# Two one-bank PSUM tiles for the second MLP's products in place of a shared two-bank tile

## The chip, the cores and the metric

The kernel runs on one core of one Trainium2 chip. A core has a tensor engine (PE, with its weight loads shown as PEld), a vector engine (DVE), a scalar engine (ACT), a GpSimd engine (POOL) and a sync engine (SP) that here issues most DMAs. Matmuls write into PSUM, 8 banks of 128 partitions by 512 fp32 values. The metric is the time of one execution on the device in microseconds; below is better.

## The reference

```python
def reference(q, k, v, moe_w_in, moe_w_out, moe2_w_in, moe2_w_out):
    # q, k, v: [8, 8, 576, 64]; w_in: [512, 2048]; w_out: [2048, 512]; all float32
    scores = q @ k.transpose(0, 1, 3, 2) / np.sqrt(64)
    ret = scores * Dmat        # causal decay gamma[h] ** (i - j), zero above the diagonal
    attn = ret @ v
    x = attn.transpose(0, 2, 1, 3).reshape(4608, 512)
    h = x @ moe_w_in
    x = (h * sigmoid(1.702 * h)) @ moe_w_out
    h = x @ moe2_w_in
    return (h - np.tanh(h)) @ moe2_w_out
```

## The kernel before

The 4608 tokens are worked in nine blocks (NB) of 512. Every product of fp32 operands is done as three matmuls of halves (PASS): each operand is split into a high part and a rest, kept side by side. The order of the instructions on each engine is the order in which the program writes them; the tile framework adds the waits, from the record of who read and wrote each tile, and hands a pool's slot to its next tile when the last one's accesses are over.

Retention (the attention part) runs first, interleaved with the first MLP. It computes in `pat`, one PSUM tile of two banks from the pool `ps_a`, and for the first blocks also in two tiles of `ps_e`. The first MLP's `mm_in` writes `h` tiles (pool `ps_h`, two banks), and its output products `mm_out` accumulate in four banks of `ps_acc`. Outputs of both MLPs are produced by one generator, `out_units`: each call of `some(outs, n)` emits n units of three matmuls (L507 for the first MLP, L509 for the second), and `evac` copies four finished accumulators out with ScalarE (L525) after every 16 steps of four units.

The second MLP's first block is done in the standard way (`mm_std`, L646). The other eight blocks go by pairs, four pairs of eight steps each, 32 steps `u` in all. A step forms seven products of combined operands (`mm_part`, L660, six matmuls each) in place of eight, and adds up four results from them. In program order a step does:

1. part 1 into x_ps, copied out as m1; then the activation of h11 of the step before (`late[0]`)
2. part 5 into y_ps, copied as m5; then the activation of the last sum of the step before (`late[1]`), which is still in PSUM, in that step's x_ps
3. part 6 added into x_ps, copied as u2 (`copied`, L866)
4. part 3 added into y_ps; h12 = y_ps + u2 (`added`, L871)
5. part 7 added into x_ps; h22 = x_ps + m5; activation of h12
6. part 2 into w_ps; h11 = w_ps + m1
7. part 4 added into x_ps; activation of h22

Output units stand between all of these. x_ps is `pat[:, u % 2]` and w_ps `pat[:, 1 - u % 2]`: the bank of w_ps in step u is that of x_ps in step u - 1, and the bank of x_ps that of w_ps. y_ps is a tile of its own from `ps_h`. An activation, `act_2`, reads its h with ScalarE (L454, L456) and VectorE (L455, L461; L461 is the last reader), and L457, L458, L460 and L462 work in SBUF. In the last but one output block, `mm_out` also uses the two halves of `pat` as its first two accumulators.

Of the kernel before, what the change touches and what calls it, by code (L numbers as in the profile page):

```python
# [8 lines left out]
F32 = mybir.dt.float32  # L9
# [8 lines left out]
P = 128  # L18
# [6 lines left out]
BLK = 512  # L25
# [23 lines left out]
def kernel(  # L49
# [18 lines left out]
    t_p = ctx.enter_context(tc.tile_pool(name="t", bufs=2))  # L68
    st_p = ctx.enter_context(tc.tile_pool(name="st", bufs=2))
    dram = ctx.enter_context(tc.tile_pool(name="dram", bufs=1, space=bass.MemoryType.DRAM))  # L70
    ps_a = ctx.enter_context(tc.tile_pool(name="ps_a", bufs=1, space=bass.MemoryType.PSUM))
    ps_h = ctx.enter_context(tc.tile_pool(name="ps_h", bufs=2, space=bass.MemoryType.PSUM))

    ctx.enter_context(tc.manual_schedule())

    early_ctx = ExitStack()
    tabs = early_ctx.enter_context(tc.tile_pool(name="tabs", bufs=1))
    at_p = early_ctx.enter_context(tc.tile_pool(name="at", bufs=2))
    qt_sb = tabs.tile([P, KD, P], F32, name="qt_sb")
# [44 lines left out]
    def dec_b(m, f, c):  # L124
        hi, _, e, z = half[m, f, c]
        nc.vector.scalar_tensor_tensor(
            out=e, in0=hi, scalar=-(2 ** 31), in1=e, op0=ALU.bitwise_and, op1=ALU.bitwise_or
        )
        del stg[m, f, c]
        o = z.bitcast(F32)  # L130
        nc.vector.tensor_tensor(out=o, in0=z.bitcast(F32), in1=e.bitcast(F32), op=ALU.mult)
        half[m, f, c] = o
        if (m, c) == (1, 0):
            part[m, f, c] = half.pop((m, f, c))

    def dec_c(m, f, c):
        if (m, c) == (1, 0):
            return
        o = half[m, f, c]
        if (m, c) == (0, 0):  # L140
            s = win[f] = wts.tile([P, 2, KD, P], F32R, tag=f"wi{f}", name="wi")
            sv = s.rearrange("p a k c -> p a (k c)")
        else:
            sv = st_p.tile([P, 2, DM], F32R, tag="ws", name="ws", bufs=2)
        nc.scalar.activation(out=sv[:, 0], in_=o, func=ACTF.Copy)
        half[m, f, c] = o, sv

    def dec_d(m, f, c):
        if (m, c) == (1, 0):
            return  # L150
        o, sv = half.pop((m, f, c))
        nc.vector.tensor_tensor(out=sv[:, 1], in0=o, in1=sv[:, 0].bitcast(F32), op=ALU.subtract)
        if (m, c) != (0, 0):
            part[m, f, c] = sv

    def dec_store():
        while part:
            (m, f, c), sv = part.popitem()
            if (m, c) == (1, 0):
                w2_d[f] = dram.tile([P, BLK], F32, tag=f"w{m}{f}{c}", name="wr")  # L160
                nc.sync.dma_start(out=w2_d[f], in_=sv)
                continue
            d = dram.tile([P, 2 * DM], F32, tag=f"w{m}{f}{c}", name="wd")
            nc.sync.dma_start(out=d, in_=sv.rearrange("p a n -> p (a n)").bitcast(F32))
            wo_d[m, f] = d
# [5 lines left out]
    def dec_load(n):  # L171
        while n_load[0] < min(n, len(chunks)):
            wload(*chunks[n_load[0]])
            n_load[0] += 1

    def dec_piece(pieces=1):

        for _ in range(pieces):
            n, k = divmod(n_dec[0], 3)
            if k == 0:  # L180
                dec_store()
            if n >= len(chunks) + 2:
                return
            n_dec[0] += 1
            if k == 0:
                dec_load(n + 2)
                if n >= 2:
                    dec_c(*chunks[n - 2])
                if 1 <= n <= len(chunks):
                    dec_b(*chunks[n - 1])  # L190
                continue
            if k == 1 and n >= 2:
                dec_d(*chunks[n - 2])
            if n < len(chunks):
                (dec_a if k == 1 else dec_a2)(*chunks[n])
# [68 lines left out]
    pat = ps_a.tile([P, 2, BLK], F32, name="pat")  # L264
# [149 lines left out]
    acc = {}  # L414
# [53 lines left out]
    second = {}  # L468
# [24 lines left out]
    def mm_out(s, m):  # L493
        j, f = divmod(s, NF)
        if f == 0:
            if j == 2 * NB - 2 and m < 2:
                acc[m] = pat[:, m]
            elif j == 2 * NB - 1 and m > 1:
                acc[m] = ps_h.tile([P, BLK], F32, tag="h", name="acc")
            else:  # L500
                acc[m] = ps_acc.tile([P, BLK], F32, tag=f"acc{m}", name=f"acc{m}")
        g, wo = gt[s], wos[s]
        c = slice(m * P, (m + 1) * P)
        for n, (a, b) in enumerate(PASS):
            first, last = f == 0 and n == 0, f == NF - 1 and n == 2
            if j < NB:
                nc.tensor.matmul(acc[m], lhsT=wo[:, a, c], rhs=g[:, b], start=first, stop=last)  # L507
            else:
                nc.tensor.matmul(acc[m], lhsT=g[:, a, c], rhs=wo[:, b], start=first, stop=last)  # L509
# [22 lines left out]
    def out_loads(o):  # L532
        while n_w[0] <= min(o + (3 if second else 2), n_steps - 1):
            wo_load()
        while n_g[0] <= min(o + (4 if second else 2), n_steps - 1):
            g_load(n_g[0])
            n_g[0] += 1
# [116 lines left out]
    def mm_part(ps, q, i, first):  # L654

        t, o = PART[i]
        n = 0
        for k in range(2):
            for a, b in PASS:
                nc.tensor.matmul(  # L660
                    ps, lhsT=wq[q][t][:, o, a, k], rhs=xo[i][k][:, b],
                    start=first and n == 0, stop=n == 5, skip_group_check=True,
                )
                n += 1
# [145 lines left out]
    for s in range(LAG, NB * NF):  # L810
        j, f = divmod(s, NF)
        o = s - LAG
        if s < PAUSE:
            out_loads(o)
        mm_in(s)
        b = EARLY + BPB + (s - LAG) // 2
        if s % 2 == 0 and b <= TILES * BPT:
            attn_step(b)
            if b == TILES * BPT:
                early_ctx.close()  # L820
                second["pool"] = ctx.enter_context(tc.tile_pool(name="second", bufs=1))
        dec_piece()
        act_a(s)
        if s < PAUSE:
            out_split(o)
        done.append(s)
        stores(2)
        if s < PAUSE:
            some(outs, 4)
        dec_piece(2 if j == 2 and f < 10 else 1)  # L830
        if n_dec[0] >= 3 * (len(chunks) + 2):
            some(prep, 1)
        if j == NB - 1 and f >= 5:
            some(std, 1)
        if j == NB - 1 and f in (11, 14):
            wq_load((f - 11) // 3, True)
# [38 lines left out]
    for u in range(pairs * QS):  # L875
        p, q = divmod(u, QS)
        ja = NB + 1 + 2 * p
        a, b = (ja * NF + q, (ja + 1) * NF + q)
        end = p == pairs - 1
        if q == 0:  # L880
            xo.update(new)
            new = {}
            ops = xo_prep(3 + 2 * p, new) if not end else iter(())
        final = q == QS - 1
        stay = iter(range(7, NF)) if end and final else iter(())

        def ready():
            if final:
                some(ops, 1)
                for f in islice(stay, 2):  # L890
                    wo_stay(f)

        n = 4 if final else 3
        x_ps, w_ps = pat[:, u % 2], pat[:, 1 - u % 2]
        y_ps = ps_h.tile([P, BLK], F32, tag="h", name="y")

        mm_part(x_ps, q, 1, True)
        m1 = copied(x_ps, "m1")
        some(outs, n)
        if late:  # L900
            act(*late[0])

        mm_part(y_ps, q, 5, True)
        m5 = copied(y_ps, "m5")
        some(outs, n)
        if late:
            act(*late[1])
        ready()

        mm_part(x_ps, q, 6, False)  # L910
        u2 = copied(x_ps, "u2")
        some(outs, n)
        if u + 1 < pairs * QS:
            wq_load((q + 1) % QS, False)
        ready()

        mm_part(y_ps, q, 3, False)
        h12 = added(y_ps, u2, "h12")
        some(outs, n)
        ready()  # L920

        mm_part(x_ps, q, 7, False)
        h22 = added(x_ps, m5, "h22")
        some(outs, n)
        act(a + QS, h12)
        ready()

        mm_part(w_ps, q, 2, True)
        h11 = added(w_ps, m1, "h11")
        some(outs, n + final)  # L930
        ready()

        mm_part(x_ps, q, 4, False)
        some(outs, 4 + final)
        act(b + QS, h22)
        if not final and q:
            some(ops, 1)
        if end and q == QS - 2:
            for f in range(3, 7):
                wo_stay(f)  # L940
        late = ((a, h11), (b, x_ps))
# [59 lines left out]
```

## Time and profile before

| | |
|---|---|
| median of 3 runs | 2001.58 us (1999.08 to 2008.21) |
| the profiled execution's own time | 1995.94 us |
| its span | 1993.9 us |
| mean granted TensorE clock | 0.945 of full speed |
| busy: PE, DVE, ACT | 1779.3, 1115.3, 875.8 us |

The profile is of one execution. Its span is 2.0 us shorter than that execution's time. PE busy time counts a matmul from its start to its modelled end, so that neighbours overlap, and a slowly clocked matmul counts as busy for longer. In a timeline, the bracket at the end of a row gives the engine's idle time just before it and the instruction that ended it.

### The profile page before, as it was taken

The numbers are of one execution on the slowest core, as the hardware profiler recorded it, in microseconds if no ns is written. First come the engines' busy times: TensorE is split into PE (matmuls) and PEld (weight loads), VectorE is DVE, ScalarE is ACT, GpSimd is POOL, SyncE is SP. The second block draws the span as 40 slices with busy tenths as digits, with TensorE's granted clock in tenths as the row PEclk, the third lists the DMA queues.
The fourth block names the chain that finished last, engine by engine and source line by source line (L and its number), as shares of the span: only waits on it lengthen the run. The fifth ranks groups of instructions, "written<-read, shape, count | busy, mean of one in ns | idle before, by whom it ended". The sixth has DMA issues, their size and how long they took to land.

```text
span 1993.9 us, 24696 instructions
## 1 busy us (share of the span) xinstructions
PE 1779.3 (89%) x8714; PEld 1431.8 (72%) x8714; DVE 1115.3 (56%) x1837; ACT 875.8 (44%) x1587; POOL 149.6 (8%) x121
## 2 busy tenths in 40 slices
PE   7998999999999999887878888888687888888889
PEld 5786888888788887776666666767575767676677
DVE  6787865565644445555455555555545565454432
ACT  3343433333333344554455444555445464444432
POOL 4100100110132101001000010000100000000000
PEclk8998999999999999998899989989889999898989
DMA  6468998888877689987667776767767576766943
GB/s 243 170 208 310 368 308 296 299 312 299 280 250 252 254 305 360 332 280 279 209 203 265 239 265 218 270 211 269 257 235 258 194 256 239 263 210 225 358 166 101
DMA packets 176025, 514.21 MB, mean 258 GB/s; under 512 B 19872, under 2 KB 21024, under 8 KB 164384
## 3 DMA queue, kind: packets, MB, share of 16 engines
q1 hardware_dynamic: 164960, 493.69, 71.0%
q10 hardware_dynamic: 10944, 18.96, 2.5%
q8 instruction: 69, 1.13, 0.2%
q14 instruction: 52, 0.43, 0.1%
HBM read 380.45 MB, written 132.12 MB: 257 GB/s over the span
## 4 chain that ended last, share of the span: by engine, by line
PE 66%; DVE 13%; ACT 10%; DMA 7%; issue 4%; ACTq 0%; SPq 0%; DVEq 0%
PE h L430 16%; PE acc L507 15%; PE acc L509 14%; PE pat L660 12%; ACT pl L457 3%; DVE pl L460 3%; DMA gd<-t 3%; DVE pl L461 3%; PE y L660 2%; ACT sq L456 2%; PE h L646 2%; PE pat L298 1%; DMA wq<-wq 1%; ACT t L454 1%; DVE t L455 1%
## 5 line engine op out<-in xcount | busy, mean ns | idle before, releaser
L507 PE MATMUL acc<-g,wos 128*128 128x512 f32 x1728 | 436.0, 401 | 6.6 <-ACT g L490 3.8
L660 PE MATMUL pat<-xo,wq 128*128 128x512 f32 x960 | 286.7, 440 | 163.7 <-DVE pl L461 141.3
L491 DVE TENSOR_TENSOR g<-gl,g 128x512 fp32r<-128x512 f32 x288 | 205.5, 715 | 373.4 <-ACT g L490 362.8
L507 PEld LDWEIGHTS acc<-g,wos 128*128 128x128 f32 x1728 | 333.4, 194 | 84.6 <-ACT o L525 4.2
L430 PE MATMUL h<-xh,wi 128*128 128x512 f32 x1152 | 378.8, 398 | 7.0 <-DVE t L440 4.7
L509 PE MATMUL acc<-wos,g 128*128 128x512 f32 x1398 | 357.7, 403 | 2.6 <-ACT o L525 2.5
L660 PEld LDWEIGHTS pat<-xo,wq 128*128 128x128 f32 x960 | 198.4, 212 | 224.2 <-ACT marks L458 114.8
L490 ACT ACTIVATE g<-gl 128x512 fp32r<-128x512 f32 x288 | 180.9, 629 | 390.9 <-PE acc L509 229.6
L509 PEld LDWEIGHTS acc<-wos,g 128*128 128x128 f32 x1398 | 276.5, 198 | 66.3 <-ACT o L525 5.6
L430 PEld LDWEIGHTS h<-xh,wi 128*128 128x128 f32 x1152 | 218.9, 190 | 60.3 <-DVE t L440 5.9
L430 PE MATMUL h<-xl,wi 128*128 128x512 f32 x576 | 226.7, 394 | 0.7 <-DVE xl L364 0.7
L440 DVE SCALAR_TENSOR_TENSOR t<-t,h 128x512 f32<-128x512 f32 x144 | 98.4, 684 | 122.0 <-ACT t L439 121.4
L460 DVE SCALAR_TENSOR_TENSOR pl<-pl,sq 128x512 f32<-128x512 f32 x144 | 101.1, 702 | 100.8 <-ACT pl L457 100.2
L439 ACT ACTIVATE t<-h 128x512 f32<-128x512 f32 x144 | 85.3, 594 | 123.8 <-DMA gd<-t 72.6
L430 PEld LDWEIGHTS h<-xl,wi 128*128 128x128 f32 x576 | 109.5, 190 | 23.0 <-DVE xl L364 1.0
L114 ACT ACTIVATE e<-e,ebias 128x512 int32<-128x512 int32 x64 | 46.3, 724 | 174.9 <-DVE e L112 174.2
L462 DVE COPY_PREDICATED t<-marks,pl 128x512 f32<-128x512 int32 x144 | 110.5, 767 | 15.2 <-ACT o L525 0.5
L457 ACT ACTIVATE pl<-sq,abias 128x512 f32<-128x512 f32 x144 | 104.1, 723 | 4.7
L458 ACT ACTIVATE marks<-sq,sbias 128x512 f32<-128x512 f32 x144 | 101.9, 708 | 0.0
L660 PE MATMUL y<-xo,wq 128*128 128x512 f32 x384 | 97.7, 390 | 0.0
L255 POOL TENSOR_TENSOR at<-at,qt_sb 128x512 f32<-128x512 f32 x35 | 47.6, 1360 | 537.3 <-DMA at<-in_attn_dram 467.0
L364 DVE TENSOR_TENSOR xl<-pat,xh 128x256 fp32r<-128x256 f32 x61 | 25.7, 422 | 108.5 <-ACT xh L363 108.3
(87 smaller groups left out, 1786.1 us busy)
## 6 DMA issues: line engine op xcount, KB each, us to landing
wos<-wd SPq DMA_DIRECT2D x262, 512.0 KB, 4.4
gd<-t SPq DMA_DIRECT2D x288, 256.0 KB, 5.0
gl<-gd SPq DMA_DIRECT2D x288, 256.0 KB, 4.4
wq<-wq SPq DMA_DIRECT2D x48, 1024.0 KB, 7.4
at<-in_attn_dram SPq DMA_DIRECT2D x33, 1024.0 KB, 6.3
stg<-in_w_dram SPq DMA_DIRECT2D x64, 512.0 KB, 6.8
wq<-wq SPq DMA_DIRECT2D x32, 768.0 KB, 9.1
wd<-ws SPq DMA_DIRECT2D x32, 512.0 KB, 6.4
```

What stands on the lines that cost most here:

```text
L430: nc.tensor.matmul(h, lhsT=win[f][:, a, k], rhs=xs[b][:, k], start=(n == 0), stop=(n == 3 * KD - 1))
L439: nc.scalar.activation(out=t, in_=h, func=ACTF.Tanh, scale=0.851)
L440: nc.vector.scalar_tensor_tensor(out=t, in0=t, scalar=1.0, in1=h, op0=ALU.add, op1=ALU.mult)
L457: nc.scalar.activation(out=pl, in_=sq, func=ACTF.Square, bias=abias)
L458: nc.scalar.activation(out=small, in_=sq, func=ACTF.Relu, bias=sbias, scale=-1.0)
L460: nc.vector.scalar_tensor_tensor(out=pl, in0=pl, scalar=CB, in1=sq, op0=ALU.add, op1=ALU.mult)
L462: nc.vector.copy_predicated(out=t, mask=small.bitcast(I32), data=pl)
L490: nc.scalar.activation(out=g[:, 0], in_=t, func=ACTF.Copy)
L491: nc.vector.tensor_tensor(out=g[:, 1], in0=t, in1=g[:, 0].bitcast(F32), op=ALU.subtract)
L507: nc.tensor.matmul(acc[m], lhsT=wo[:, a, c], rhs=g[:, b], start=first, stop=last)
L509: nc.tensor.matmul(acc[m], lhsT=g[:, a, c], rhs=wo[:, b], start=first, stop=last)
L660: nc.tensor.matmul(ps, lhsT=wq[q][t][:, o, a, k], rhs=xo[i][k][:, b], start=first and n == 0, stop=n == 5, skip_group_check=True,)
```

## The change

The pool `ps_a` with `pat` moves to the other side of PSUM and into the context that closes with retention. When it closes, a pool `ps_x` opens there, with two tags x0 and x1 of one bank each. Each step takes a tile for x_ps from tag x(u % 2) at its start, and one for w_ps from tag x(1 - u % 2) just before part 2. The last but one output block takes its first two accumulators from the same tags.

```diff
@@ pools
-    ps_a = ctx.enter_context(tc.tile_pool(name="ps_a", bufs=1, space=bass.MemoryType.PSUM))
     ps_h = ctx.enter_context(tc.tile_pool(name="ps_h", bufs=2, space=bass.MemoryType.PSUM))
 
     ctx.enter_context(tc.manual_schedule())
 
     early_ctx = ExitStack()
+    ps_a = early_ctx.enter_context(tc.tile_pool(name="ps_a", bufs=1, side="right", space=bass.MemoryType.PSUM))
@@ mm_out
             if j == 2 * NB - 2 and m < 2:
-                acc[m] = pat[:, m]
+                acc[m] = second["psum"].tile([P, BLK], F32, tag=f"x{m}", name="acc")
@@ end of retention
                 early_ctx.close()
                 second["pool"] = ctx.enter_context(tc.tile_pool(name="second", bufs=1))
+                second["psum"] = ctx.enter_context(tc.tile_pool(name="ps_x", bufs=1, side="right", space=bass.MemoryType.PSUM))
@@ loop of the seven products
         n = 4 if final else 3
-        x_ps, w_ps = pat[:, u % 2], pat[:, 1 - u % 2]
+        x_ps = second["psum"].tile([P, BLK], F32, tag=f"x{u % 2}", name="x")
         y_ps = ps_h.tile([P, BLK], F32, tag="h", name="y")
 
         mm_part(x_ps, q, 1, True)
...
         act(a + QS, h12)
         ready()
 
+        w_ps = second["psum"].tile([P, BLK], F32, tag=f"x{1 - u % 2}", name="w")
         mm_part(w_ps, q, 2, True)
         h11 = added(w_ps, m1, "h11")
```

## Rows read from the trace of the kernel before

**Rows 1.** The page: busy us, share of the span and instructions of each engine.
```profile
PE 1779.3 (89%) x8714; PEld 1431.8 (72%) x8714; DVE 1115.3 (56%) x1837; ACT 875.8 (44%) x1587; POOL 149.6 (8%) x121
```

**Rows 2.** Busy time by stretches, with granted clock, DMA share and GB/s last.
```profile
200.00:250.00 50.00, 50.00 (x308) 41.41 (x308) 41.78 (x77) 20.45 (x39) 5.06 (x4) 1.00 0.99 370
280.00:560.00 280.00, 278.20 (x1666) 226.00 (x1665) 170.67 (x321) 101.73 (x207) 32.69 (x28) 1.00 0.85 298
690.00:842.00 152.00, 142.45 (x608) 114.94 (x606) 79.44 (x119) 71.98 (x124) 13.09 (x8) 0.98 0.91 330
842.00:866.58 24.58, 24.58 (x108) 20.35 (x109) 10.78 (x17) 8.98 (x17) 0.00 (x0) 1.00 0.82 290
842.00:1890.00 1048.00, 883.23 (x3552) 707.50 (x3552) 559.24 (x826) 512.39 (x870) 30.40 (x12) 0.92 0.72 248
```

**Rows 3.** Groups by line, 842 to 1900 us: busy, mean ns, idle before, releasers.
```profile
L660 PE MATMUL pat<-xo,wq 128*128 128x512 f32 x960 | 286.7, 440 | 163.7 <-DVE pl L461 141.3 <-DVE h L871 20.7 <-DMA wq<-wq 1.7
...
L525 ACT ACTIVATE o<-acc 128x512 f32<-128x512 f32 x48 | 28.6, 596 | 18.2 <-ACT o L525 11.7 <-PE acc L509 4.0 <-PE y L660 1.0
```

**Rows 4.** Who waited for whom, 842 to 1900 us: total us, times, longest.
```profile
PE pat L660 <- DVE pl L461: 141.3, 31, 10.0
...
PE pat L660 <- DVE h L871: 20.7, 16, 2.5
```

**Rows 5.** Timeline of PE, products of the first and second step.
```profile
848.90 1.52 PE L660 MATMUL pat<-xo,wq 128*128 128x512 f32 x6
...
855.70 1.52 PE L660 MATMUL pat<-xo,wq 128*128 128x512 f32 x6
...
859.10 1.52 PE L660 MATMUL pat<-xo,wq 128*128 128x512 f32 x6
...
866.58 1.52 PE L660 MATMUL pat<-xo,wq 128*128 128x512 f32 x6
...
877.76 2.90 PE L660 MATMUL pat<-xo,wq 128*128 128x512 f32 x6 [4.22 <-DVE pl L461]
```

**Rows 6.** Timeline of all engines through one step: start us, us, engine, line.
```profile
1267.74 1.29 PE L509 MATMUL acc<-wos,g 128*128 128x512 f32 x5
...
1272.05 0.71 ACT L458 ACTIVATE marks<-sq,sbias 128x512 f32<-128x512 f32 x1
...
1272.90 0.69 DVE L461 SCALAR_TENSOR_TENSOR pl<-pl,pat 128x512 f32<-128x512 f32 x1
...
1273.74 2.90 PE L660 MATMUL pat<-xo,wq 128*128 128x512 f32 x6 [4.71 <-DVE pl L461]
...
1276.67 0.60 ACT L866 ACTIVATE u<-pat 128x512 f32<-128x512 f32 x1 [3.91 <-PE pat L660]
...
1285.40 1.52 PE L660 MATMUL pat<-xo,wq 128*128 128x512 f32 x6
...
1289.55 0.67 DVE L871 TENSOR_TENSOR h<-pat,m 128x512 f32<-128x512 f32 x1
...
1290.27 1.65 PE L660 MATMUL pat<-xo,wq 128*128 128x512 f32 x6 [1.31 <-DVE h L871]
...
1294.48 1.52 PE L660 MATMUL pat<-xo,wq 128*128 128x512 f32 x6
```

**Rows 7.** The chain that ended last: a stretch of nine matmuls.
```profile
1280.12 2.04 PE acc L509 x9
```

**Rows 8.** Timeline of PE: four waits, in the stage before, loop and tail.
```profile
778.61 4.47 PE L646 MATMUL h<-xo,wq 128*128 128x512 f32 x12 [3.96 <-DMA wq<-wq]
...
801.84 2.65 PE L507 MATMUL acc<-g,wos 128*128 128x512 f32 x6 [2.44 <-ACT o L525]
...
1444.61 2.93 PE L660 MATMUL pat<-xo,wq 128*128 128x512 f32 x6 [10.01 <-DVE pl L461]
...
1900.10 2.90 PE L509 MATMUL pat<-wos,g 128*128 128x512 f32 x6 [9.79 <-ACT t L454]
```

**Rows 9.** Who waited for whom, 690 to 842 us.
```profile
PE h L646 <- DMA wq<-wq: 5.4, 3, 4.0
```

## The prediction

> **What bounds the kernel now.** I began with the busy shares [rows 1]: TensorE is at 89% of the span and no other engine is above 72% (its own weight loads), so the question is where the missing tenth of TensorE lies. The table by stretches answers it [rows 2]. From 280 to 560 us TensorE is busy 278.20 of 280 us at a granted clock of 1.00. The loop over the second MLP's seven products, 842 to 1890 us, has it busy 883.23 of 1048 us at a mean granted clock of 0.92: over half of the span, and nearly all of the loss. The reader is to see two losses there: 164.8 us of idle time, and a busy time that is itself too long.
>
> The second loss is sized with the price of a matmul. Nine at full pace take 2.04 us [rows 7], 0.2267 us each. The loop has 3552 of them [rows 2], so 805.2 us would do, and 883.2 − 805.2 = 78.0 us are slow pace. The clock's two levels are 2.4 and 1.2 GHz; 0.92 is a mixture. The pace falls right behind idle time: six matmuls after an idle 4.71 us take 2.90 us [rows 6], where 6 × 0.2267 = 1.36 us is full pace; after an idle 1.31 us they take 1.65 us.
>
> Then, who ends the idle time. The matmuls of L660 into the tile pat have 163.7 us of it in front of them [rows 3], 141.3 us ended by the vector engine's L461 in 31 waits and 20.7 us by its L871 in 16 [rows 4]. Of 164.8 us only some 3 us are anything else.
>
> Last, which data this wait is for. In the timeline of one ordinary step [rows 6] the third product (part 6, into half u%2 of pat) is next in TensorE's queue when the outputs' matmuls end at 1267.74 + 1.29 = 1269.03 us. It starts at 1273.74, 0.15 us after L461 has finished reading pat at 1272.90 + 0.69 = 1273.59. But that L461 belongs to the activation of the step before, which reads half 1 − u%2. The same shows at 1290.27: the seventh product, into half u%2, starts when L871's h11, a reader of the other half, ends at about 1290.23. Twice a product waits for a reader of a bank it doesn't write; what the two share is the tile. Two more things bear this out. The first step has no activation left over, and its part 6 starts at 848.90 without idle time, while the second step's, at 877.76, waits 4.22 us for L461 [rows 5]. And that first step takes 24.58 us for its 108 matmuls, at clock 1.00 [rows 2], where the mean of the loop's 32 steps is 1048/32 = 32.75 us for 3552/32 = 111.
>
> **The change, part by part.** No instruction of an engine or queue is added, removed or put in another order: matmuls, activations and DMAs are the same. What changes is which waits they carry.
>
> *The tile's place* (pat on the other side of PSUM, closed with retention): retention still has one tile of two banks, in the same order. Cost nothing: between retention and the first use of the new tiles at 842 us lies the stretch from 690 us on in which only other products run [rows 2], and it covers the hand-over. Without that cover it would be one wait for the last reader.
>
> *Separate tiles.* Part 6 then depends, on this side, only on the copy m1 that read its own bank, over before 1269 us. The 141.3 us go. The seventh product no longer waits for h11 but only for h22, over several microseconds earlier; the 20.7 us go. With the idle time goes the slow pace behind it, up to 78.0 us. Ceiling: 141.3 + 20.7 + 78.0 = 240 us.
>
> *What is late next.* I lay the step of [rows 6] out anew with the spacing of the unhindered step [rows 5]. Part 6 at 1269.03. Part 7 is due 855.70 − 848.90 = 6.80 us later, at 1275.83, and waits for u2, the copy of part 6's sum. ScalarE takes u2 behind the leftover activation, whose last piece ends at 1272.05 + 0.71 = 1272.76; u2 needs 0.60 us: 1273.4. Slack 2.4 us. Part 2 (w_ps, whose bank the leftover activation reads) is due 859.10 − 848.90 = 10.20 us after part 6, at 1279.23; the reader ends at 1273.59. Slack 5.6 us: this is the real dependency, and it is ample. The next step's first product reuses w's bank and waits for h11: due 866.58 − 859.10 = 7.48 us after part 2, so 1292.88 if part 2 starts at 1285.40 as now; h11 ends at 1290.23. Slack 2.65 us. So an ordinary step would be about the first step's 24.6 us.
>
> Not all steps are ordinary. At 1444.61 the wait is 10.01 us [rows 8], the longest of the 31; the slack there is 2.4 − (10.01 − 4.71) = −2.9 us, so part 7 waits 2.9 us there. I take 4 us for this and its like in all; the lower end is nothing, and the upper end is the first rival's 34.
>
> *Evacuations.* Twelve fall in the loop (48 copies, [rows 3]). With fewer pauses, more of them will hold TensorE up. Bounds: nothing each, as nearly all now, and 2.44 us each, the one at 801.84 [rows 8]. I take the middle, 1.2 us, 14 us in all; ends 0 and 29.
>
> *Transfers.* 248 GB/s over 1048 us are 260 MB; in 805 us that asks for 323 GB/s. From 200 to 250 us the queues moved 370 GB/s and TensorE was busy all 50 us at clock 1.00: price nothing. The stretch 690 to 842 us moved 330 GB/s and lost 5.4 us to loads of wq [rows 9]; over 805 us that would be 29 us. The loop's first step, which has the same loads, moved 290 GB/s without a wait, and 323 lies between: nearer nothing, I take 5 us.
>
> *Pace behind these waits.* After 3.96 us idle, 12 matmuls took 4.47 us in place of 2.72; after 2.44 us, six took 2.65 in place of 1.36 [rows 8]: about half the wait again. (14 + 4 + 5) × 1.5 = 34 us.
>
> *The tail.* At 1900.10 a product waits 9.79 us for the last readers of pat [rows 8]. The first accumulator of that block then gets the tile that w used, free by then; the second gets the one still being read. Three matmuls move forward, 0.7 us; counted as nothing.
>
> Loop: 805 + 34 = 839 us, 209 us less. From the profiled execution's own 1995.94 us that is 1787 us. The median of the runs, 2001.58, lies 0.28% above that execution; with the same factor, 1792 us.
>
> A rule to weigh against this: the Trainium skill, "PSUM — Partial Sum Buffer", section "PSUM bank collisions raise a hardware error", wants accesses guarded by bank and quadrant, and says that different banks run clean. By it the wait on the other bank guards nothing and can go; the trace's start 0.15 us behind a reader of the other bank shows a wait that is stricter than that.
>
> **The rivals.**
>
> *The wait moves to part 7.* ScalarE is busy 512 us of 1048 now; in 839 us that is 61%, VectorE 67%. If the leftover activation ends 3.5 us later in each step against part 6 than it does now, part 7 waits 1.1 us in each of 31, 34 us, with slow pace 51, less the 6 counted (4 × 1.5): 1792 + 45 = 1837 us. For it: both engines work strictly in their order, and the slack is only 2.4 us. Against: the engine that was late mostly waited for TensorE itself.
>
> *Transfers bind.* At the 290 GB/s of the loop's first step, 260 MB take 897 us in place of 839: 1850 us. Against it: 370 GB/s beside a fully busy TensorE.
>
> *The change does not do what it says.* If L461's wait has another cause than the shared tile, nothing moves: 1996 to 2002 us. Against it: the two cross-bank waits and the first step without one. The Trainium skill has a case that points this way: "TensorE: Matmul & The Clock Gate", section "HAM oscillation — how this bites in real kernels", reports that more PSUM buffers gave a kernel no further gain. By that the time stays about 2000 us. There it was transfers that held the matmuls; here the row names a reader of PSUM.
>
> *Slower.* The hand-over of a bank between tiles could cost more than the wait it replaces: the first product of each step now takes a tile over from w, whose reader h11 stands in VectorE's queue behind a whole activation. If h11 came so late that each of 32 steps lost over 240/32 = 7.5 us, that is 2.65 + 7.5 = 10.2 us later than now, the kernel would be slower; at 12 us later it loses 9.4 × 32 − 240 = 59 us, 2060 us. Against: the same reader precedes the same bank's next writer today, without idle time in front of the first product (1294.48).
>
> **How the numbers follow.** Forecast 0.76, part 7 0.11, transfers 0.06, no effect 0.05, slower 0.02. The likeliest gives 1792 us. Its own range: down to 1763 with only 5 us of the 34 paid, up to 1830 with the evacuations at their upper end and half of the upper price of wq (29 + 4 + 15, times 1.5, is 72, 38 more than counted). To leave out no more than 2 in 10 the range reaches over the first two rivals to 1855. Faster by over 0.5% (about what a measurement of this kernel can tell from no change): 0.76 + 0.11 + 0.06 = 0.93; within it 0.05; slower 0.02.
>
> **What would show it.** Right: no idle time in front of L660 ended by L461 or by h11; steps of about 24.6 us; the granted clock in the loop near 0.98; the loop's matmuls in 830 to 860 us; transfers above 300 GB/s. The first rival: ScalarE's u2 late, idle time in front of part 7 ended by L866. The second: idle time ended by transfers of wq, gl or wos, with landings above 10 us. Wrong altogether: part 6 still starting behind L461.

## The result, and the profile after

The changed kernel takes 1766.62 us in the median (1758.21 to 1767.13, 4 runs) against 2000.33 us (the three runs of the section on the kernel before, and one more), 234 us less. The ratio over the runs is 0.8817, 95% interval 0.8779 to 0.8854, so 11.8% less. The forecast was 1792 us, in a range of 1763 to 1855; the mechanism was the forecast one, its side costs were put too high.

The page after, the lines that answer to [rows 1], and the granted clock in 40 slices:

```profile
span 1765.1 us, 24667 instructions
...
PE 1702.7 (96%) x8714; PEld 1388.0 (79%) x8714; DVE 1116.6 (63%) x1837; ACT 870.0 (49%) x1587; POOL 150.7 (9%) x121
...
PEclk8999999999999999999999999999999999999899
```

The matmuls are the same 8714, and VectorE's and ScalarE's busy times are those of before within 6 us: no work went away, waits did. The stretches, which answer to the first, third and last of [rows 2] (the loop now ends at about 1661 us):

```profile
560.00:690.00 130.00, 130.00 (x842) 106.37 (x841) 61.12 (x121) 49.03 (x106) 31.27 (x36) 1.00 0.70 248
690.00:842.00 152.00, 143.68 (x611) 115.97 (x610) 79.19 (x118) 71.89 (x123) 13.09 (x8) 0.98 0.90 331
842.00:1661.00 819.00, 811.43 (x3552) 667.08 (x3550) 559.64 (x826) 505.85 (x869) 31.61 (x12) 1.00 0.91 316
...
1661.00:1765.00 104.00, 89.36 (x383) 73.15 (x381) 30.23 (x45) 31.50 (x51) 0.00 (x0) 0.93 0.46 152
```

Everything before the loop and the tail behind it (1890 to 1994 before, 104 us both times) last as long as they did. The loop's gain, 1048 − 819 = 229 us, is the whole gain of the two profiled executions (1995.94 against 1767.13 us): its idle time fell from 164.8 to 7.6 us, its busy time from 883.2 to 811.4 at a granted clock of 1.00. Who waited for whom, 842 to 1665 us, against [rows 4]:

```profile
PE x L660 <- DVE h L872: 3.2, 1, 3.2
...
PE acc L509 <- ACT o L525: 2.4, 4, 1.1
...
PE acc L507 <- ACT o L525: 1.3, 1, 1.3
...
PE x L660 <- ACT u L867: 0.4, 1, 0.4
```

No product of the loop waits for L461 any more. The timeline of all engines shows why that is no accident of timing; x at 1230.40 is part 6, and L461 is the last reader of the other tile named x:

```profile
1230.40 1.52 PE L660 MATMUL x<-xo,wq 128*128 128x512 f32 x6
...
1231.31 0.60 ACT L456 ACTIVATE sq<-x 128x512 f32<-128x512 f32 x1 [0.95 <-DVE t L455]
...
1233.43 0.69 DVE L461 SCALAR_TENSOR_TENSOR pl<-pl,x 128x512 f32<-128x512 f32 x1
...
1234.23 0.58 ACT L867 ACTIVATE u<-x 128x512 f32<-128x512 f32 x1
```

Part 6 starts 3.7 us before that reader is done (1233.43 + 0.69 = 1234.12); before, it started 0.15 us behind it. ScalarE's wait of `sq` for VectorE's `t`, two readers of one and the same bank, is still there. It is no wait for data, since `sq` doesn't use `t`: where h lies in SBUF, as h12 does here, the same `sq` starts long before that `t`:

```profile
955.83 0.62 ACT L456 ACTIVATE sq<-h 128x512 f32<-128x512 f32 x1
...
964.73 0.68 DVE L455 TENSOR_TENSOR t<-h,t 128x512 f32<-128x512 f32 x1
```

### The profile page after: what moved, and what is told of

Same layout as the page of the kernel before. It is cut to its first block, busy times and chain, and to the rows that moved or that the text cites. A ratio compares the mean times of both kernels' runs of the same rounds, so it can differ in the third digit from the quotient of the medians.

```text
span 1765.1 us, 24667 instructions
## 1 busy us (share of the span) xinstructions
PE 1702.7 (96%) x8714; PEld 1388.0 (79%) x8714; DVE 1116.6 (63%) x1837; ACT 870.0 (49%) x1587; POOL 150.7 (9%) x121
## 4 chain that ended last, share of the span: by engine, by line
PE 80%; DVE 7%; DMA 7%; ACT 4%; issue 2%; SPq 0%; ACTq 0%; DVEq 0%
PE acc L509 20%; PE acc L507 19%; PE h L430 18%; PE x L660 9%; PE y L660 4%; PE w L660 2%; DMA gd<-t 2%; PE h L646 2%; PE pat L298 2%; DMA wq<-wq 1%; DMA gl<-gd 1%; PE pat L349 1%; PE pat L284 1%; DVE t L440 1%; PE pat L313 1%
## 5 line engine op out<-in xcount | busy, mean ns | idle before, releaser
L507 PE MATMUL acc<-g,wos 128*128 128x512 f32 x1728 | 426.1, 394 | 7.2 <-ACT g L490 3.8
L507 PEld LDWEIGHTS acc<-g,wos 128*128 128x128 f32 x1728 | 324.4, 189 | 81.7 <-ACT o L525 5.6
L509 PE MATMUL acc<-wos,g 128*128 128x512 f32 x1416 | 347.9, 392 | 13.2 <-DVE pl L461 10.7
L491 DVE TENSOR_TENSOR g<-gl,g 128x512 fp32r<-128x512 f32 x288 | 213.0, 740 | 201.7 <-ACT g L490 196.3
L490 ACT ACTIVATE g<-gl 128x512 fp32r<-128x512 f32 x288 | 180.6, 628 | 301.4 <-PE acc L509 150.8
L509 PEld LDWEIGHTS acc<-wos,g 128*128 128x128 f32 x1416 | 266.7, 189 | 72.2 <-DVE pl L461 11.1
L660 PE MATMUL x<-xo,wq 128*128 128x512 f32 x768 | 196.8, 392 | 4.1 <-DVE h L872 3.2
L660 PEld LDWEIGHTS x<-xo,wq 128*128 128x128 f32 x768 | 144.6, 189 | 35.9 <-DVE h L872 3.8
```

Source lines behind the costliest of these rows:

```text
L490: nc.scalar.activation(out=g[:, 0], in_=t, func=ACTF.Copy)
L491: nc.vector.tensor_tensor(out=g[:, 1], in0=t, in1=g[:, 0].bitcast(F32), op=ALU.subtract)
L660: nc.tensor.matmul(ps, lhsT=wq[q][t][:, o, a, k], rhs=xo[i][k][:, b], start=first and n == 0, stop=n == 5, skip_group_check=True,)
```

## Experiments

The theory: the waits come from two banks being one tile, and what they cost is their length and the slow pace behind them. The rivals: the place or lifetime of the pool; a need of part 6 for that reader; transfers close to binding.

**One tile in the new pool.** Only the split into two tiles is taken back.

```diff
+    second["two"] = second["psum"].tile([P, 2, BLK], F32, name="two")
-    x_ps = second["psum"].tile([P, BLK], F32, tag=f"x{u % 2}", name="x")
+    x_ps, w_ps = second["two"][:, u % 2], second["two"][:, 1 - u % 2]
-    acc[m] = second["psum"].tile([P, BLK], F32, tag=f"x{m}", name="acc")
+    acc[m] = second["two"][:, m]
```

> The pools move as in the change, but the loop takes one two-bank tile from the new pool and slices it as before. Theory (the waits come from the two banks being one tile): about 2000 us, ratio 0.99 to 1.01, again some 141 us of idle time in front of part 6 ended by L461 and some 21 us in front of part 4 ended by h11. Rival (the place or the lifetime of the pool made the gain): about 1767 us, ratio 0.88.

Measured: 1999.22 us, ratio 0.9993 (0.9973 to 1.0013). Its waits of PE in the loop:

```profile
PE two L660 <- DVE pl L461: 144.5, 31, 10.0
...
PE two L660 <- DVE h L873: 20.8, 16, 2.5
```

They are [rows 4] again, in the new pool and place. The split is the whole gain; where the pool lies gives nothing beyond the 0.3% that the interval leaves open.

**The orders alone, with one tile.** The leftover activation (`late[1]`, which still reads the other half) is written behind part 6 (first run), h11 behind part 4 (last run), or both (run between).

```diff
         some(outs, n)
+        mm_part(x_ps, q, 6, False)
         if late:
             act(*late[1])
         ready()
-        mm_part(x_ps, q, 6, False)
...
         mm_part(w_ps, q, 2, True)
-        h11 = added(w_ps, m1, "h11")
         some(outs, n + final)
-        ready()
         mm_part(x_ps, q, 4, False)
+        h11 = added(w_ps, m1, "h11")
+        ready()
```

> One two-bank tile, but the leftover activation is written behind part 6 in the program; the order on ScalarE and VectorE stays. Theory: part 6 no longer waits, since that reader is recorded later; part 7, due 6.8 us after part 6, finds L461 done. Left are the 16 or so waits for h11 of 1.3 us with 0.3 us of slow pace each, 26 us: about 1793 us, ratio 0.896. Rival (part 6 really needs that reader to be over, or the wait moves to part 7): 1900 to 2000 us.

> As the run before, and h11 is written behind part 4. Theory: with both readers recorded later, one two-bank tile is as good as two: 1767 us within 8, ratio 0.878 to 0.887. Rival (two tiles give something that order cannot): at least 20 us slower than the changed kernel.

> One two-bank tile, with only h11 written behind part 4. Theory: the small term alone, 20.7 us of waits and 5 us of slow pace: about 1974 us, ratio 0.987; the 141 us ended by L461 stay. Rival (the two waits are one chain, and what is gained at part 4 is waited for again at the next part 6): 1995 to 2000 us.

| written later | median us | ratio, 95% interval |
|---|---|---|
| leftover activation | 1815.14 | 0.9068 (0.9039 to 0.9097) |
| both | 1785.17 | 0.8915 (0.8883 to 0.8947) |
| h11 | 1975.75 | 0.9861 (0.9828 to 0.9894) |

The last fits in time: 2002.58 − 1975.75 = 27 us for the small term, expected 26. Its trace agrees only in part: h11 ends no wait any more, but the loop is no more than 18 us shorter (1029.9 us against 1048.3, from the first product to the wait in the tail). L461's waits are no fewer, and one wait, for h22, is new. Some of what h11 gave may be waited for again, as the rival had it; these runs don't settle how much:

```profile
PE two L660 <- DVE pl L461: 147.3, 31, 8.0
...
PE two L660 <- DVE h L873: 5.3, 1, 5.3
```

The first shows that part 6 has no need of the reader: written ahead of it, part 6 no longer waits and 187 us go. But both runs with that order missed their numbers, the first by 22 us, and the one with both orders came out 18 us above the mark, between theory and rival. The expectation had it that the order on ScalarE stays. It does, but ScalarE now waits. Timeline of the run with both orders, around an evacuation:

```profile
945.43 1.52 PE L660 MATMUL two<-xo,wq 128*128 128x512 f32 x6
...
946.99 0.60 ACT L454 ACTIVATE t<-two 128x512 f32<-128x512 f32 x1 [2.09 <-PE two L660]
...
951.18 0.60 ACT L868 ACTIVATE u<-two 128x512 f32<-128x512 f32 x1 [0.87 <-DVE pl L461]
...
952.32 1.65 PE L507 MATMUL acc<-g,wos 128*128 128x512 f32 x3 [4.00 <-ACT o L525]
```

and of the changed kernel, at the same place of the program:

```profile
945.11 0.58 ACT L454 ACTIVATE t<-x 128x512 f32<-128x512 f32 x1
...
948.80 0.57 ACT L867 ACTIVATE u<-x 128x512 f32<-128x512 f32 x1
...
949.91 0.96 PE L507 MATMUL acc<-g,wos 128*128 128x512 f32 x3 [1.30 <-ACT o L525]
```

The leftover activation, a reader of one half, now waits for part 6 into the other half, and u2 on ScalarE waits for VectorE's L461, again a reader of the other half. The evacuation behind them comes later and holds TensorE for 4.00 us in place of 1.30. So the shared tile ties reader to writer and reader to reader, whichever stands first; an order only chooses who waits. In the loop, TensorE's waits there are:

```profile
PE acc L507 <- ACT o L525: 5.8, 2, 4.0
...
PE acc L509 <- ACT o L525: 4.9, 4, 1.8
...
PE two L660 <- DVE h L873: 3.4, 4, 1.8
...
PE two L660 <- ACT u L868: 3.2, 5, 1.4
```

Those for evacuations sum to 10.7 us (3.7 in the changed kernel), those for u2 to 3.2 (0.4): 10 of the 15 us by which that loop is longer (835 us against 820, from the first product to the wait in the tail). Most of the rest is pace: over these stretches TensorE is busy 817.3 us in place of 813.0 for the same part of the program. In the run with only the leftover activation moved, the waits that L873 ends (for h11 or h22) are also more than expected, 23.8 us in 22.

**More bytes in the loop.** Each of 176 output steps also copies its 256 KB within memory.

```diff
+        if 80 <= s < 256:
+            spare = dram.tile([P, BLK], F32, tag=f"spare{s}", name="spare")
+            nc.sync.dma_start(out=spare, in_=gd[s])
```

> The changed kernel with one more transfer of 256 KB, from memory to memory, for each of the 176 output steps of the loop: 46 MB more, 305 MB in all in the loop. Theory (TensorE binds the loop, the transfers have room up to the 370 GB/s seen from 200 to 250 us): the loop grows by no more than 20 us. Rival (at 316 GB/s and a share of 0.91 the transfers are already what binds): the loop grows with the bytes, by 80 us or more, with idle time in front of matmuls that loads of wq, wos or gl end.

Measured: 1775.32 us, ratio 0.8879 (0.8853 to 0.8906), 9 us more than the changed kernel's 1765.91 (0.8823, 0.8798 to 0.8849) on the same chip. The loop, in the columns of [rows 2]:

```profile
842.00:1661.00 819.00, 807.14 (x3526) 658.63 (x3524) 553.74 (x819) 500.44 (x862) 33.53 (x12) 1.00 0.98 368
```

At 368 GB/s and a share of 0.98 TensorE is still busy 807 of 819 us. In the whole loop (842 to 1670 us) loads end only two of its waits, 2.6 us, both loads of wos. The transfers have about the room that the 370 GB/s of [rows 2] showed, and at 316 GB/s they do not bind.

**The tail.** As in [rows 8], a product of the tail waits some 10 us for the last activations; in the changed kernel it is the first product of the second accumulator. First another bank for it, then also two output steps written ahead of the activations, then also a buffer of its own for the fourth evacuated accumulator (which shares five with h11, h12 and h22).

```diff
+            if (j, m) in ((2 * NB - 2, 0), (2 * NB - 1, 3)):
+                acc[m] = second["psum"].tile([P, BLK], F32, tag=f"x{int(m > 0)}", name="acc")
+            elif (j, m) in ((2 * NB - 2, 1), (2 * NB - 1, 2)):
                 acc[m] = ps_h.tile([P, BLK], F32, tag="h", name="acc")
...
+    some(outs, 8)
     for n in late[::-1]:
         act(*n)
-    some(outs, 4)
...
-            if second and m < 3:
-                parts.append(second["pool"].tile([P, BLK], F32, tag="o", name="o", bufs=3))
+            if second:
+                parts.append(second["pool"].tile([P, BLK], F32, tag="o", name="o", bufs=4))
...
-        more = {"t": 3, "gl": 2, "g": 1}[what]
+        more = {"t": 2, "gl": 2, "g": 1}[what]
```

> The changed kernel once more, as the measure for the next two on the same chip: 1766 us within 6, ratio 0.878 to 0.886.

> The changed kernel, but the second accumulator of the last but one output block takes a free bank of the y tiles in place of the bank that the last activation still reads, and the last block's fourth accumulator takes that one. Theory (the 10.65 us in front of the tail's matmuls are the wait for that one reader, and slow pace behind it): the wait goes, 10 to 13 us less than the changed kernel, about 1755 us. Rival (ScalarE's copies or the splits of g, behind the same activations, are late next and hold the same matmuls): 0 to 4 us less.

> As the run with the other bank in the tail, and the fourth evacuated accumulator gets a buffer of its own kind in place of one of the five that h11, h12, h22 and the copies share (one buffer of t is given up for the room). Theory (the 3.18 us wait of part 4 for h22 came from h22 waiting 8.27 us for a buffer until an evacuation had landed): 4 to 8 us less than the run with the tail alone. Rival (one t buffer fewer makes the activations wait for their stores): as slow as or slower than the tail alone.

> The run with the other bank in the tail, and two output steps are written ahead of the two last activations, so that ScalarE has the next splits of g done before it turns to them. Theory (in that run the wait was not gone because the splits stood behind the activations): the 6.38 us in front of the tail's matmuls go, about 8 us less than the changed kernel, 1757 us. Rival (something further behind holds the tail, its loads of g above all): no less than 1762 us.

> The same with the buffer of its own for the fourth evacuated accumulator. Theory: both gains add up, 11 to 14 us less than the changed kernel, about 1753 us, ratio 0.876. Rival (the buffer's gain is not real): as the run with the order alone.

| kernel | median us | ratio, 95% interval |
|---|---|---|
| changed kernel again | 1765.91 | 0.8823 (0.8798 to 0.8849) |
| other bank | 1764.36 | 0.8822 (0.8797 to 0.8846) |
| other bank, buffer | 1760.90 | 0.8802 (0.8775 to 0.8829) |
| other bank, order | 1759.27 | 0.8797 (0.8783 to 0.8812) |
| other bank, order, buffer | 1753.66 | 0.8767 (0.8746 to 0.8787) |

The other bank alone gives nothing that can be told from noise, as the rival had it. PE's timeline of the changed kernel, and then of the one with the other bank:

```profile
1672.00 10.13 PE L509 MATMUL acc<-wos,g 128*128 128x512 f32 x33 [10.65 <-DVE pl L461]
```

```profile
1658.44 4.79 PE L509 MATMUL acc<-wos,g 128*128 128x512 f32 x18 [0.96 <-ACT o L525]
1669.62 1.22 PE L509 MATMUL acc<-wos,g 128*128 128x512 f32 x2 [6.38 <-ACT g L490]
1671.66 4.25 PE L509 MATMUL acc<-wos,g 128*128 128x512 f32 x10 [0.82 <-DVE g L491]
```

Twenty-one matmuls come forward, the eighteen of the first row among them, and then the splits of g (L490 and L491, which make the two halves of an output operand), behind the same activations, are late. With the order changed as well, the wait for L490 is 2.75 us, and a load of wos holds a product for 1.30 us:

```profile
1667.17 3.00 PE L509 MATMUL acc<-wos,g 128*128 128x512 f32 x12 [1.30 <-DMA wos<-wd]
...
1675.63 0.89 PE L509 MATMUL acc<-xo,g 128*128 128x512 f32 x2 [2.75 <-ACT g L490]
```

With the order added 6.6 us go, a little under the 8 expected, and with the buffer added 3.5 us against the other bank, under the 4 to 8 expected; both intervals still overlap the changed kernel's, so neither is settled by itself. Together they are 0.6% faster than the changed kernel, 12.3 us of the 11 to 14 expected, with intervals that don't meet (the two were timed on different occasions, each against the kernel before; with the first four runs of the changed kernel, 0.8779 to 0.8854, they overlap a little). The wait of part 4 that the buffer was meant for, 3.18 us at 964.27 in the changed kernel's timeline, does not appear in either run with it. Its h22 stood 8.27 us before it could start, until the store of an evacuated accumulator had landed:

```profile
963.52 0.69 DVE L872 TENSOR_TENSOR h<-x,m 128x512 f32<-128x512 f32 x1 [8.27 <-DMA x<-o]
...
964.27 2.93 PE L660 MATMUL x<-xo,wq 128*128 128x512 f32 x6 [3.18 <-DVE h L872]
```

## Why the prediction was right, and where it was off

*The cause*: right. The cross-bank waits were waits of a shared tile; one tile in the new pool brings back 144.5 and 20.8 us, two tiles take both away.

*The ceiling* of 240 us: right. The loop stood 243 us over the 805.2 us that its matmuls need, and 229 of them were recovered. The slow pace went with the idle time: 78.0 us became 811.4 − 805.2 = 6.2.

*What is late next*: right for ordinary steps. Part 2's real dependency never shows as a wait, and part 7 waited for u2 once, 0.4 us (twice, 1.7 us, when the changed kernel ran again). A step took 819/32 = 25.6 us in the mean; the 24.6 us of the prediction are a step of 108 matmuls, and 111 need 25.2 at 0.2267 us each. The first rival, at 0.11, did not come.

*The side costs*: this is the step that was mis-sized. Against the 34 us of "(14 + 4 + 5) × 1.5" stand 13.8: the 14 us for evacuations were 3.7; 4 us for part 7 were 0.4, with 3.2 for an h22 that waited for its buffer, which the prediction had not seen; 5 us for loads were nothing; 11 us of pace were 6.2. The middle between nothing and 2.44 us each was too dear for the evacuations: in the loop before, twelve of them had held matmuls for some 2.5 us in all, and that row, not the single 2.44 us of the stage before, was the nearest:

```profile
PE acc L509 <- ACT o L525: 2.5, 4, 1.1
```

*The median*: the factor of 1.0028 added 5 us. The changed kernel's median is no higher than its profiled execution. The two together, 20 and 5, are the 25 us between 1792 and 1767.

*Transfers*: the price of nothing from the stretch at 370 GB/s was the right end: at 316 GB/s no product of the loop after 842 us waited for a load. The lost time of the stage from 690 us on is that stage's own. *The tail*: nothing, as counted.

*The slower rival*: the first product of a step, which takes over w's bank, waits for h11 nowhere in the loop.

## What to carry to other kernels

Look at which part of a tile the releasing instruction reads. Where a matmul starts right behind a reader of another bank, the wait may be for the tile, and giving each bank a tile of its own is the test; here it took the wait away. Moving the readers behind the writers in the program recovered most of it here (217 of 234 us), but the tie between the halves stayed and moved to the readers' engines. For matmuls, count a pause with the slow pace behind it: here 162 us of cross-bank waits in the trace stood behind a gain of 229.

## What the runs showed of the hardware

In the run with more bytes the transfers went at 368 GB/s, with a share of 0.98, through the 819 us from 842 to 1661 us beside a TensorE that was busy 98.6% of them. And in the changed kernel 7.6 us of scattered idle time left the granted clock of the loop at 1.00, where one wait of 4.6 us in the mean in each step (141.3 us in 31) had gone with 0.92; the prediction had looked for 0.98.
